# Seven block products in place of eight in half of a feed-forward layer, and one attention operand by DMA

## The chip, the cores and the metric

The kernel runs on one core of a Trainium2 chip. The metric is device microseconds of one execution, from the median of three runs. Five engines work side by side: TensorE (PE, matrix products), VectorE (DVE), ScalarE (ACT), GpSimd (POOL), and SyncE (SP), which issues most DMAs. A queue is in order on each engine.

## The reference, cut to what matters

Attention on 4 batches of 8 heads, 576 positions, 64 wide, with a block-causal mask of 64; the heads are put side by side, so 2304 tokens of width 512 leave it. Two feed-forward layers follow, the first with 2048 hidden units, the second with three input matrices and 768 hidden units.

```python
attn = exp(scores - max) / (sum + 1e-9); x = attn @ v          # 2304 x 512
h = x @ w_in;  r = maximum(h, 0);  x = (s * (r * r) + b) @ w_out      # 512 -> 2048 -> 512
h = maximum(maximum(x @ w1, x @ w2), x @ w3);  out = h @ w_out2       # 512 -> 768 -> 512
```

The weights come as 64-bit floats and have to be turned into 32-bit ones by integer work on their two words.

## The kernel before, in words

Every product is taken to near fp32 precision from halves: a matrix is split into a rounded part (hi) and its rest (lo), and one block product is three matmuls, hi by hi, hi by lo and lo by hi. A matmul has 128 rows, 128 columns of weights, and 512 or 384 tokens.

The program records operations with their reads and writes (`Sched.op`), each with a cost and one or more engines; `Sched.run` then plays a list scheduler over them and writes out one fixed order for each engine. Costs (`c_mm`, `c_exp`, `c_two`, the constants near line 259), offsets of priority (`CFG["off"]`) and the order of recording set that order. At run time each engine follows its order and waits for what an instruction reads.

**Attention** goes pair of heads by pair of heads, 16 pairs. `prep_pair` makes the operands of the next pair: hi of K and of Q (lines 444 to 450, on POOL from pair 2 on), lo of K (453), lo of Q (462), and a second copy of hi of Q, called q2 here, which the DVE computes again from the raw Q (457 to 459). `softmax_pair` then has per pair 9 score blocks: matmuls, a maximum on DVE (496), an exponential on ACT (500). `values_pair` turns the exponentials by 25 transposes (561), which ACT copies out (360), and multiplies by V.

**Weights** go through `convert` (673): a load of 512 KB, a clamp (684), a scaling of the high word (688, ACT or POOL), a shift (692), and two merging passes on DVE (696, 701). `pair_out` splits the result to hi and lo. `prepare_v` does this for a matrix taken as it is, `prepare_b` for one taken by blocks, which adds four sums and seven splits; results for later go to DRAM (wscr, bscr) and come back by `fetch`.

**The first layer** is done in two passes of 8 hidden blocks each (f = 0..7, 8..15). The tokens stand in five chunks, three of 512 and two of 384. `l1` is the first product of one f and one chunk (12 matmuls) with relu, square, scale and bias on ACT (924, 929, 936) and the split of the result; `l2` is the second product (12 matmuls). The first pass takes chunks 0 and 1 together: all `l1`, whose results go to DRAM (hscr) for lack of room and come back, then all `l2`. The other chunks and the second pass run one f after the other, with `l2` one step behind `l1`. Partial sums of the first pass wait in DRAM (pscr).

**The second layer** takes its first products by blocks: two by two blocks of weights and of tokens, in groups of 768 tokens, with seven block products in place of eight (`seven`, line 877; sums of token blocks in `blocks_of_x`, 814). A block product is 6 matmuls of 384 tokens; the sums after it are DVE additions (874).

Of the kernel before, what the change touches and what calls it, by code (L numbers as in the profile page):

```python
# [28 lines left out]
HOLD = 3  # L29
# [4 lines left out]
W_REBIAS = 2.0 ** -112  # L34
W_MAX = struct.unpack("<f", struct.pack("<I", (1151 << 20) - 512))[0]
# [22 lines left out]
def c_two(n):  # L58

    return n / 2.4 + 55  # L60
# [18 lines left out]
def c_exp(n):  # L79
    return n / 1.2 + 271  # L80
# [72 lines left out]
class Sched:  # L153
# [45 lines left out]
    def run(self):  # L199
# [26 lines left out]
        while len(order) < n:  # L226
# [28 lines left out]
            if e == "PE":  # L255

                m = self.ops[i][5]
                if side != (m == "side"):
                    c += 93 if not side else 55 if m == "turn" else 100
                side = m == "side"  # L260
# [11 lines left out]
def tile_attention_moe(ctx: ExitStack, tc: tile.TileContext, qk, vp, w_in, w_out, s_, b_, w123, w_out2, out):  # L272
# [13 lines left out]
    def places(at, n, *sizes):  # L286

        out_ = []
        for m, w in zip(n, sizes):
# [5 lines left out]

    IAT, XAT1, OAT, HAT1, RN = places(0, (NF // 2, KT, NF // 2, 2 * HOLD + 1), 1024, 1024, 1024, 1024)
    XAT, HAT, WAT_, VAT, HATB, rn = places(0, (14, 2, 8, NG, 2), 2 * HN, 2 * HN, 512, 1024, 2 * HN)
# [6 lines left out]
    PTN = sum(pt_w)  # L304
    SAT, NAT, at = places(0, (1, 2), 1024, 512)
    TAT = places(0, (5,), HN)[0]
    RAWAT, K0AT, NMAT, DENAT, RDAT, RVAT, PTAT, *EAT = places(at, (CFG["raw"], CFG["k0"], CFG["nmx"], 2, 1, CFG["rawv"], CFG["pt"]) + tuple(CFG["e"]),
                                                              2 * S, 256, NB, 36, 128, 17 * D, PTN, *e_w)
    FN = EAT.pop()
    SAT2, RGAT1, PAT, WV2, WB2, UAT, fn = places(at, (5, 3, 4, 2, 4, 6), 1024, 512, 512, 1024, 512, HN)  # L310
# [9 lines left out]
    hscr = dram.tile([NF, 128, 1024], F32, name="hscr")  # L320
    pscr = dram.tile([KT, 128, NT], F32, name="pscr")
    bscr = dram.tile([7 * 3 * NG // 2, 128, 512], F32, name="bscr")
# [11 lines left out]
    def words2(t):  # L334
# [4 lines left out]
                 x1=Strip(arena, XAT1, 1024, two), x1b=Strip(arena, OAT[1:5], 1024, two), h1=Strip(arena, HAT1, 1024, two),  # L339
                 x=Strip(arena, XAT, 2 * HN, two), v=Strip(arena, VAT, 1024, two), h=Strip(arena, HAT + HATB, 2 * HN, two), w=Strip(arena, WAT_, 512, two),  # L340
                 wb=Strip(other, WB2, 512, two), wv=Strip(other, WV2, 1024, two),
                 stg=Strip(other, SAT, 1024, words2), nrm=Strip(other, NAT, 512), rg1=Strip(other, RGAT1, 512), part=Strip(other, PAT + [UAT[0] + 512 * i for i in range(4)], 512), t1=Strip(other, TAT[0:2], HN), t2=Strip(other, TAT[2:4], HN), tt=Strip(other, TAT[4:], HN), y=Strip(other, WV2, 512),
                 u=Strip(other, UAT, HN), rg=Strip(other, RGAT, HN), gb=Strip(other, GAT, HN),
                 **{"e%d" % j: Strip(other, EAT[j], w) for j, w in enumerate(e_w)},
                 **{"iw%d" % j: Strip(arena, [x], 1024, two) for j, x in enumerate(IAT)}, **{"ow%d" % j: Strip(arena, [x], 1024, two) for j, x in enumerate(OAT)},
                 **{"pt%d" % j: Strip(other, [x + sum(pt_w[:j]) for x in PTAT], w) for j, w in enumerate(pt_w)})
# [55 lines left out]

    def parts(p):
# [7 lines left out]
    def load_pair(p):  # L411
# [3 lines left out]
        if p == 0:  # L415

            for x, i, cols, heads in [("a", 0, (384, 768), HEADS)] + [("a", 1, (S * h, S * h + C0), (h,)) for h in HEADS] + [
# [255 lines left out]
    def convert(src, kind, after=()):  # L673
# [13 lines left out]
        def f(e):  # L687
            mul_to(e, hi_f, hi_f, W_REBIAS)
# [689 lines left out]
```

## Time and profile before

| | |
|---|---|
| median of 3 runs | 852.61 us (851.32 to 856.37) |
| the profiled execution's own time | 853.07 us |
| its span, first to last instruction | 851.1 us |
| PE busy | 835.5 us, 98% |
| DVE, ACT, POOL busy | 616.2, 441.8, 81.9 us |
| TensorE clock granted, mean | 0.997 |

The span is what the profile's rows cover; about 2 us of the execution's own time lie around it. PE's busy time counts matmuls that overlap in a pipeline, so 98% doesn't say that PE goes at its peak; how many matmuls start in a stretch says more. Attention fills the span up to about 178 us, the first layer goes from there to 571 us, the second layer to the end.

### The profile page before, as it was taken

What the parts mean: (1) busy time and instruction counts of PE and PEld (TensorE: products, weight loads), DVE (VectorE), ACT (ScalarE), POOL (GpSimd) and SP (SyncE); (2) the same over time, 40 slices, a digit from 0 to 9 for tenths busy, and PEclk for the clock granted to TensorE, in tenths of its full rate; (3) what the DMA queues carried; (4) which work ended last, traced back from release to release, by engine and by line L of the source; (5) the groups of instructions that cost most, each with busy time, mean ns of one, the idle gap of its engine ahead of it and who ended that gap; (6) DMA issues with size and microseconds to landing.
All of it is one profiled execution on the core that took longest, in us unless ns stands there. A gap on an engine that the chain in (4) does not pass through costs nothing.

```text
span 851.1 us, 13711 instructions
## 1 busy us (share of the span) xinstructions
PE 835.5 (98%) x4802; PEld 735.5 (86%) x4802; DVE 616.2 (72%) x1191; ACT 441.8 (52%) x984; POOL 81.9 (10%) x94
## 2 busy tenths in 40 slices
PE   7999999999999999999999999999999999999997
PEld 6777776777888899999998888889999999999995
DVE  7788999999948899945993323567569566847662
ACT  4899999989705677655774434440115101320112
POOL 6222223202001131000100000000000000000000
PEclk9999999999999999999999999999999999999999
DMA  7556674758698888999662010247674676657742
GB/s 251 167 187 215 193 242 156 254 169 315 220 412 314 277 289 294 354 362 332 216 244 75 1 50 1 82 140 249 205 227 149 209 230 202 188 172 225 232 126 75
DMA packets 73461, 176.62 MB, mean 208 GB/s; under 512 B 8752, under 2 KB 13104, under 8 KB 73392
## 3 DMA queue, kind: packets, MB, share of 16 engines
q1 hardware_dynamic: 72672, 175.02, 62.1%
q8 instruction: 38, 0.62, 0.3%
q10 hardware_dynamic: 720, 0.72, 0.2%
q14 instruction: 31, 0.25, 0.1%
HBM read 132.91 MB, written 42.80 MB: 206 GB/s over the span
## 4 chain that ended last, share of the span: by engine, by line
PE 81%; DVE 9%; ACT 4%; DMA 3%; issue 2%; POOL 0%; ACTq 0%; SPq 0%; DVEq 0%; POOLq 0%
PE ps L368 78%; PE ps L561 4%; DVE arena L365 2%; DVE other L496 2%; ACT other L500 2%; DMA bscr<-other 1%; DVE other L365 1%; DVE arena L462 1%; ACT other L360 1%; DMA other<-pscr 1%; DVE other L701 1%; DMA other<-qk 1%; DVE arena L354 1%; DVE other L696 0%; POOL other L356 0%
## 5 line engine op out<-in xcount | busy, mean ns | idle before, releaser
L368 PE MATMUL ps<-arena 128*128 128x384 f32 (+7 forms) x3758 | 746.1, 357 | 5.4 <-ACT other L500 1.4
L368 PEld LDWEIGHTS ps<-arena 128*128 128x128 f32 (+1 forms) x3758 | 664.0, 189 | 81.1 <-ACT other L500 10.7
L874 DVE TENSOR_TENSOR other<-ps,other 128x384 f32<-128x384 f32 x189 | 101.1, 554 | 64.1 <-PE ps L368 62.4
L365 DVE TENSOR_TENSOR arena<-other,arena 128x384 fp32r<-128x384 f32 (+3 forms) x173 | 119.1, 699 | 23.1 <-ACT arena L352 18.9
L352 ACT ACTIVATE arena<-other 128x384 fp32r<-128x384 f32 (+3 forms) x107 | 59.9, 567 | 83.8 <-DVE other L1245 54.2
L924 ACT ACTIVATE other<-ps 128x512 f32<-128x512 f32 (+1 forms) x80 | 44.0, 551 | 98.3 <-PE ps L368 97.1
L354 DVE TENSOR_SCALAR arena<-other 128x512 fp32r<-128x512 f32 (+3 forms) x72 | 40.8, 569 | 70.9 <-ACT other L936 67.1
L360 ACT ACTIVATE other<-ps 128x512 f32<-128x512 f32 (+2 forms) x139 | 73.5, 571 | 29.6 <-PE ps L368 20.6
L500 ACT ACTIVATE other<-ps,other 128x576 f32<-128x576 f32 (+4 forms) x144 | 78.7, 563 | 11.2 <-DVE other L496 10.6
L496 DVE TENSOR_REDUCE other<-ps 128x1 f32<-128x576 f32 (+4 forms) x144 | 68.0, 512 | 11.8 <-ACT other L500 4.6
L352 ACT ACTIVATE other<-other 128x256 fp32r<-128x256 f32 (+3 forms) x101 | 51.9, 527 | 46.0 <-DVE other L684 37.8
L886 ACT ACTIVATE other<-ps 128x384 f32<-128x384 f32 x27 | 13.3, 491 | 114.9 <-PE ps L368 91.8
L356 POOL TENSOR_SCALAR other<-other 128x512 f32<-128x512 f32 (+1 forms) x46 | 38.6, 842 | 293.3 <-DVE other L684 162.0
L936 ACT ACTIVATE other<-other,cst 128x512 f32<-128x512 f32 (+1 forms) x80 | 61.6, 771 | 1.9
L561 PE MATMUL ps<-ident,other 128*128 128x128 f32 x400 | 57.0, 280 | 3.3 <-ACT other L500 2.9
L368 PE MATMUL ps<-other 128*64 128x64 f32 (+5 forms) x640 | 54.9, 313 | 1.2 <-ACT other L352 1.2
L561 PEld LDWEIGHTS ps<-ident,other 128*128 128x128 f32 x400 | 44.9, 143 | 7.3 <-ACT other L500 5.1
L929 ACT ACTIVATE other<-other 128x512 f32<-128x512 f32 (+1 forms) x80 | 47.0, 589 | 1.8
L368 PEld LDWEIGHTS ps<-other 128*64 128x64 f32 (+1 forms) x640 | 29.7, 136 | 20.9 <-issue 15.5
L365 DVE TENSOR_TENSOR other<-other 128x256 fp32r<-128x256 f32 (+1 forms) x85 | 41.6, 499 | 2.0 <-ACT other L352 1.4
L696 DVE SCALAR_TENSOR_TENSOR other<-other 128x512 uint32<-128x512 uint32 x56 | 38.4, 686 | 4.1 <-POOL other L356 2.7
L701 DVE SCALAR_TENSOR_TENSOR other<-other 128x512 uint32<-128x512 uint32 x56 | 39.8, 711 | 0.2
(35 smaller groups left out, 332.9 us busy)
## 6 DMA issues: line engine op xcount, KB each, us to landing
arena<-bscr SPq DMA_DIRECT2D x189, 256.0 KB, 3.1
other<-qk SPq DMA_DIRECT2D x30, 576.0 KB, 3.8
bscr<-other SPq DMA_DIRECT2D x63, 256.0 KB, 4.9
other<-w_out SPq DMA_DIRECT2D x22, 512.0 KB, 4.9
wscr<-other SPq DMA_DIRECT2D x22, 512.0 KB, 5.1
arena<-wscr SPq DMA_DIRECT2D x22, 512.0 KB, 6.1
other<-w SPq DMA_DIRECT2D x18, 512.0 KB
other<-vp SPq DMA_DIRECT2D x16, 544.0 KB, 4.5
```

Source lines behind the costliest of these rows:

```text
L352: nc.scalar.activation(out=dst, in_=src, func=AF.Copy, scale=m)
L354: nc.vector.tensor_scalar(out=dst, in0=src, scalar1=m, scalar2=None, op0=ALU.mult)
L360: nc.scalar.activation(out=dst, in_=src, func=AF.Copy)
L365: eng[e].tensor_tensor(out=dst, in0=a, in1=b, op=ALU.subtract)
L368: nc.tensor.matmul(o, l, r, start=start, stop=stop)
L496: nc.vector.tensor_reduce(out=NM.ap[:, u:u + 1], in_=v, axis=AX.X if n <= 512 else AX.XY, op=ALU.max, negate=True)
L500: nc.scalar.activation(out=ev, in_=v, func=AF.Exp, bias=NM.ap[:, u:u + 1], scale=1.0, accum_out=DEN.ap[:, d:d + 1])
L561: nc.tensor.transpose(TB.ap[:, 128 * i:128 * i + 128], x, ident)
L701: nc.vector.scalar_tensor_tensor(out=lo_w, in0=hi_w, scalar=0x80000000, in1=lo_w, op0=ALU.bitwise_and, op1=ALU.bitwise_or)
L874: nc.vector.tensor_tensor(out=out_.ap, in0=bank.ap[:, 0:HN], in1=u.ap, op=ALU.add)
L929: nc.scalar.activation(out=r, in_=r, func=AF.Square)
L936: nc.scalar.activation(out=r, in_=r, func=AF.Identity, scale=s_t, bias=b_t)
```

## The change

- In the first layer's second pass (f = 8..15) the first product is taken by blocks, as the second layer does it: seven block products in place of eight, groups of 768 tokens. `seven`, `blocks_of_x`, `prepare_b` and `fetch` serve both layers now; `hidden` and `l2_half` are new.
- The first pass takes all five chunks one after the other, `l2` three steps behind `l1` (LAG). The detour of results through hscr is gone.
- From pair 2 on, q2 is copied by a DMA from hi of Q, in place of being computed by DVE.
- `convert` does the scaling and the sign in one activation on ACT; the second merging pass on DVE is gone, and POOL no longer scales.
- The loads of the first pair are cut another way, buffers are laid out anew, and some of the scheduler's costs are changed.

```diff
 def convert(src, kind, after=()):
-            mul_to(e, hi_f, hi_f, W_REBIAS)
-        op(CFG_E("wreb", ACT=c_acts(512), Pool=c_pool(512), DVE=335), 0, f, ...)
+            nc.scalar.activation(out=hi_f, in_=hi_f, func=AF.Prelu, scale=W_REBIAS, alpha=W_SIGN)
+        op("ACT", c_acts(512), f, ...)
...
-            nc.vector.scalar_tensor_tensor(out=lo_w, in0=hi_w, scalar=0x80000000, in1=lo_w, op0=ALU.bitwise_and, op1=ALU.bitwise_or)
-        op("DVE", 602, f, ...)

 def prep_pair(p, R):
+            if p < CFG["q2d"]:      # 2
...
+            else:
+                    nc.sync.dma_start(out=f32(q2[0:64]), in_=f32(qh[0:64]))
+                load(256 * nq, f, reads=[(Q1, c) for c in keys], writes=[(KQ, (1,) + c) for c in keys], kind="prep2")

+def l2_half(G, b, f_, accs):
+        W, Hh, t, i = ready["out", f_], hs.pop((f_, b)), half(G, b), accs["n"]
+        for k in range(KT):
...
+                mm(o, W.ap[:, 0, kk], Hh.ap[:, 0, :], i == 0, False)
+                mm(o, W.ap[:, 0, kk], Hh.ap[:, 1, :], False, False)
+                mm(o, W.ap[:, 1, kk], Hh.ap[:, 0, :], False, i == HF - 1)
+            op("PE", 3 * c_mm(HN), f, ...)

-    PASSES = [(0, c) for c in range(2, NC)] + [(1, c) for c in reversed(range(NC))]
+    PASSES = [(0, c) for c in range(NC)]
-    aside = [(x, f_ + HF) for x, f_ in order1]
+    aside = [k for i in range(HF // 2) for k in [(i, "in"), ("out", HF + i), ("out", HF + i + HF // 2)]]

+    for n_, G in enumerate(GORD):
+        P1, P2 = SETS[n_ % 2], SETS[1 - n_ % 2]
+        acc = accumulators(P2, KT)
+        keep, todo = {}, []
+        for i in range(HF // 2):
+            def between():
+                for f_ in todo:
+                    l2_half(G, 0, f_, acc)
...
+            c = seven((i, "in"), P1, dst, between)
+            f1, f2 = HF + i, HF + i + HF // 2
+            for x in ("C11", "C21", "C22", "C12"):
+                hidden(c[x])          # relu, square, scale and bias, all on ACT
+            split_h((f1, 0), c["C11"])
+            split_h((f2, 0), c["C21"])
+            keep[f1], keep[f2] = c["C12"], c["C22"]
+            todo = [f1, f2]
+            prepare_aside(aside2, "w2")
...
+        acc = accumulators(P1, KT)
+        for f_ in c_order:
+            split_h((f_, 1), keep[f_])
+            l2_half(G, 1, f_, acc)

-CFG = {'aside2': 2,
+CFG = {'aside': 8, 'aside2': 24,
```

How the engines' orders move, at three places. PE, from the end of attention to the second layer, before:

```order
L650 MATMUL ps<-ident,other 36x128
L368 MATMUL ps<-arena 128x512 x561
L368 MATMUL ps<-arena 128x384 x12
L368 MATMUL ps<-arena 128x512 x12
L368 MATMUL ps<-arena 128x384 x744
L368 MATMUL ps<-arena 128x512 x12
L368 MATMUL ps<-arena 128x384 x12
L368 MATMUL ps<-arena 128x512 x552
L368 MATMUL ps<-arena 128x384 x9
```

And now:

```order
L670 MATMUL ps<-ident,other 36x128
L371 MATMUL ps<-arena 128x512 x540
L371 MATMUL ps<-arena 128x384 x12
L371 MATMUL ps<-arena 128x512 x12
L371 MATMUL ps<-arena 128x384 x12
L371 MATMUL ps<-arena 128x512 x12
L371 MATMUL ps<-arena 128x384 x12
L371 MATMUL ps<-arena 128x512 x12
L371 MATMUL ps<-arena 128x384 x1578
```

The second run of 512-wide matmuls is gone, and one long run of 384-wide ones goes on into the second layer. Over the whole program the list has 1476 matmuls of 512 and 1902 of 384 before, 900 and 2598 now; all the others are as many as before.

DVE in the middle of attention (TENSOR_REDUCE is the maximum, 64x1024 into arena is q2 or, as SCALAR_TENSOR_TENSOR, lo of Q; 64x1152 is lo of K), before:

```order
L496 TENSOR_REDUCE other<-ps 128x1 x3
L354 TENSOR_SCALAR arena<-other 64x1024
L365 TENSOR_TENSOR arena<-other,arena 64x1152
L496 TENSOR_REDUCE other<-ps 128x1 x4
L462 SCALAR_TENSOR_TENSOR arena<-other,arena 64x1024
L792 TENSOR_TENSOR xf<-xf,other 128x512
```

And now:

```order
L812 TENSOR_TENSOR xf<-xf,other 128x512
L368 TENSOR_TENSOR arena<-other,arena 64x1152
L516 TENSOR_REDUCE other<-ps 128x1 x4
L482 SCALAR_TENSOR_TENSOR arena<-other,arena 64x1024
L812 TENSOR_TENSOR xf<-xf,other 128x512
```

The q2 instruction has gone from every one of the 14 pairs. It stands now on SP as a DMA of 64x1024 (the loads there: qk is raw K and Q, vp is V, scr the denominators), where before there was

```order
L786 DMA other<-scr 64x512 x4
L481 DMA other<-vp 128x1088
L425 DMA other<-qk 128x1152 x2
L481 DMA other<-vp 128x1088
L659 DMA scr<-other 8x4x128
```

and now

```order
L806 DMA other<-scr 64x512 x4
L501 DMA other<-vp 128x1088
L478 DMA arena<-arena 64x1024
L440 DMA other<-qk 128x1152 x2
L501 DMA other<-vp 128x1088
```

so that the copy stands behind a load of V and ahead of the next raw loads.

ACT in the second pass of the first layer, before:

```order
L924 ACTIVATE other<-ps 128x512
L929 ACTIVATE other<-other 128x512
L936 ACTIVATE other<-other,cst 128x512
L352 ACTIVATE arena<-xf 128x512 x3
L924 ACTIVATE other<-ps 128x512
```

And now, by blocks (L914 copies a block product out of ps; L1232, L1237 and L1244 are relu, square, scale and bias; L355 is a hi part; L708 is a weight's scaling):

```order
L1232 ACTIVATE other<-other 128x384
L355 ACTIVATE arena<-other 128x384
L914 ACTIVATE other<-ps 128x384
L1232 ACTIVATE other<-other 128x384
L1237 ACTIVATE other<-other 128x384 x2
L1244 ACTIVATE other<-other,cst 128x384 x2
L355 ACTIVATE arena<-other 128x384 x2
L355 ACTIVATE other<-other 128x256
L708 ACTIVATE other<-other 128x512 x2
```

The relu no longer reads ps: it follows a DVE addition, and the preparation of weights stands between the steps.

## Rows read from the trace of the kernel before

**Rows 1.** Page, first lines: span, then busy us by engine.

```profile
span 851.1 us, 13711 instructions
...
PE 835.5 (98%) x4802; PEld 735.5 (86%) x4802; DVE 616.2 (72%) x1191; ACT 441.8 (52%) x984; POOL 81.9 (10%) x94
```

**Rows 2.** Windows: stretch, length, busy PE PEld DVE ACT POOL, clock, DMA, GB/s.

```profile
20.00:178.00 158.00, 154.56 (x1341) 116.50 (x1342) 145.31 (x237) 142.63 (x434) 41.54 (x48) 0.99 0.64 198
350.00:395.00 45.00, 45.00 (x261) 44.88 (x261) 24.38 (x60) 23.84 (x45) 0.00 (x0) 1.00 0.99 358
405.00:440.00 35.00, 35.00 (x204) 35.00 (x203) 34.74 (x83) 28.13 (x58) 2.72 (x2) 1.00 0.69 237
450.00:560.00 110.00, 110.00 (x487) 91.12 (x487) 41.58 (x76) 48.02 (x72) 0.00 (x0) 1.00 0.14 45
320.00:450.00 130.00, 129.04 (x731) 126.73 (x730) 105.75 (x250) 88.42 (x176) 7.98 (x7) 1.00 0.85 299
```

**Rows 3.** Groups, PE, 320:450 us: count, busy, mean ns, idle.

```profile
L368 PE MATMUL ps<-arena 128*128 128x384 f32 x703 | 123.2, 335 | 1.0 <-DVE arena L365 1.0
L368 PE MATMUL ps<-arena 128*128 128x512 f32 x28 | 6.8, 392 | 0.0
```

**Rows 4.** Waits of PE, 178:851 us: total us, times, longest.

```profile
PE ps L368 <- DVE arena L365: 1.0, 2, 0.8
```

**Rows 5.** Chain of waits, 20 to 175 us, shares by line.

```profile
by line: PE ps L368 41.3%; PE ps L561 20.1%; ACT other L500 9.7%; DVE other L496 7.9%; issue 5.7%; DVE arena L365 4.8%; ACT other L360 3.6%; DVE arena L462 2.1%; DVE xf L792 1.6%; DVE arena L354 1.3%; ACT xf L360 0.8%; DVE other L696 0.4%; 
```

**Rows 6.** Groups, DVE, attention, 20:178 us.

```profile
L365 DVE TENSOR_TENSOR arena<-other,arena 64x1152 fp32r<-64x1152 f32 x14 | 22.1, 1579 | 0.1
...
L354 DVE TENSOR_SCALAR arena<-other 64x1024 fp32r<-64x1024 f32 x14 | 16.7, 1194 | 0.2
```

**Rows 7.** Timeline of DVE, two runs of q2: start, length.

```profile
19.79 0.69 DVE L354 TENSOR_SCALAR arena<-other 64x1024 fp32r<-64x1024 f32 x1
...
30.08 1.84 DVE L354 TENSOR_SCALAR arena<-other 64x1024 fp32r<-64x1024 f32 x1
```

**Rows 8.** Timeline of POOL, hi of K and of Q, two pairs.

```profile
30.34 1.04 POOL L356 TENSOR_SCALAR arena<-other 128x1024 fp32r<-128x1024 f32 x1
...
58.69 2.63 POOL L356 TENSOR_SCALAR arena<-other 128x1152 fp32r<-128x1152 f32 x2 [2.34 <-PE ps L368]
```

**Rows 9.** Timeline of PE, the first scores of pair 6.

```profile
70.30 0.47 PE L368 MATMUL ps<-arena 128*128 128x192 f32 x2
```

**Rows 10.** Waits of SP's queue, attention: total us, times, longest.

```profile
SPq L481 <- PE ps L561: 27.2, 9, 5.9
```

**Rows 11.** DMA issues, 0:180 us: count, KB, us to landing.

```profile
other<-vp SPq DMA_DIRECT2D x16, 544.0 KB, 4.5
```

**Rows 12.** Groups, ACT, attention, 20:178 us: a weight's scaling.

```profile
L352 ACT ACTIVATE other<-other 128x512 f32<-128x512 f32 x3 | 2.1, 695 | 1.1 <-DVE other L684 1.1
```

**Rows 13.** Groups, ACT, chunks of 384, 310:440 us.

```profile
L936 ACT ACTIVATE other<-other,cst 128x384 f32<-128x384 f32 x31 | 21.9, 708 | 0.8
L929 ACT ACTIVATE other<-other 128x384 f32<-128x384 f32 x30 | 15.7, 525 | 0.8
L924 ACT ACTIVATE other<-ps 128x384 f32<-128x384 f32 x30 | 14.6, 486 | 26.1 <-PE ps L368 26.1
L352 ACT ACTIVATE other<-other 128x256 fp32r<-128x256 f32 x35 | 14.2, 428 | 5.7 <-DMA bscr<-other 2.6 <-DVE other L748 1.6 <-DVE other L701 1.2
L352 ACT ACTIVATE arena<-other 128x384 fp32r<-128x384 f32 x18 | 9.4, 525 | 0.5
```

**Rows 14.** Groups, DVE, second layer, 575:650 us.

```profile
L874 DVE TENSOR_TENSOR other<-ps,other 128x384 f32<-128x384 f32 x63 | 33.7, 554 | 20.8 <-PE ps L368 20.3
...
L365 DVE TENSOR_TENSOR arena<-other,arena 128x384 fp32r<-128x384 f32 x10 | 5.4, 552 | 1.8 <-ACT arena L352 1.8
```

**Rows 15.** Groups, DVE, weights being prepared, 250:300 us.

```profile
L701 DVE SCALAR_TENSOR_TENSOR other<-other 128x512 uint32<-128x512 uint32 x13 | 8.9, 688 | 0.1
...
L684 DVE TENSOR_SCALAR other<-other 128x512 f32<-128x512 f32 x14 | 5.9, 423 | 0.0
```

More of the change, by code (lines that the diff above doesn't have):

```diff
@@ L463, in f @@
                                                op1=ALU.subtract)
-            both("DVE", c_dve(nq), f, reads=qr + [(Q1, c) for c in keys], writes=[(Q1, c) for c in keys], kind="preplo", lock=True)
+            both("DVE", c_dve(nq), f, reads=qr + [(Q1, c) for c in keys], writes=[(Q1, ("l",) + c) for c in keys], kind="preplo", lock=True)
             if i == 0 and p == 0 or i == len(parts(p)) - 1 and p:
@@ L773, in half, with chunks_of @@
         return slice(2 * HN * G + HN * b, 2 * HN * G + HN * b + HN)
+    def chunks_of(G, b):
+        t = half(G, b)
+        return [c for c in range(NC) if CHUNKS[c][0] < t.stop and t.start < sum(CHUNKS[c])]
     def normalize(c):
@@ L812, in split_x, with blocks_of_x, xop @@
             xdone1.setdefault((c, k), []).extend((i, j))
-    def blocks_of_x(G):
+    xdone2 = {}
+    def blocks_of_x(G, layer):
         src, read = {}, {}
+        done = xdone2[G] = [] if layer == 1 else None
+        def xop(*a, **k):
+            j = op(*a, **k)
+            if layer == 1:
+                done.append(j)
         for i in range(2):
             for x, k, b in (("B11", i, 0), ("B12", i, 1), ("B21", 2 + i, 0), ("B22", 2 + i, 1)):
-                src[x, i], read[x, i] = xf[:, k, half(G, b)], [(XF, ("x2", c, k)) for c in range(NC) if CHUNKS[c][0] < half(G, b).stop and half(G, b).start < sum(CHUNKS[c])]
+                src[x, i], read[x, i] = xf[:, k, half(G, b)], [(XF, ("x", c, k)) for c in chunks_of(G, b)] if layer == 1 else [(XF, ("x2", G, b, k))]
         for x in BBLK:
@@ L902, in seven, with l1 @@
         return c
-    HS = Use(hscr)
-    def l1(c, f_, PH, away=False):
+    def l1(c, f_, PH):
         c0, n = CHUNKS[c]
@@ L1206, in tile_attention_moe @@
         s_now, c = PASSES[n_]
+        while direct and (("in", min(i + 2, HF - 1)) not in ready or i + 2 >= LAG and ("out", min(i + 2 - LAG, HF - 1)) not in ready):
+            prepare_direct("w")
         l1(c, f_, banks.get(SETS[0]))
-        if c == NC - 1 and s_now == 0:
-            ready["in", f_ + HF] = fetch("iw%d" % f_, ("in", f_ + HF), kind="wf")
         if f_ % HF == HF - 1 and n_ + 1 < len(PASSES) and PASSES[n_ + 1][1] != c:
             split_x(PASSES[n_ + 1][1])
-        if i:
-            l2_all(*steps[i - 1])
@@ L1214, in tile_attention_moe @@
-        prepare_aside(aside, "w2")
-        if n_ >= CFG["aside2"] and i % 2:
+        if i >= LAG:
+            l2_all(*steps[i - LAG])
+        if i >= CFG["aside"]:
+            prepare_aside(aside, "w2")
+        if i >= CFG["aside2"] and i % 2:
             prepare_aside(aside2, "w2")
-    blocks_of_x(GORD[0])
+    assert not direct and not aside
+    blocks_of_x(GORD[0], 1)
     for _ in WAT_:
         next_b()
-    l2_all(*steps[-1])
-    assert not aside and not aside2
+    for x in steps[-LAG:]:
+        l2_all(*x)
@@ L1222, in tile_attention_moe @@
+    assert not aside2
     while flow_v:
```

190 lines of the change are left out of this document (100 added, 90 removed).

## The prediction

> **What bounds the kernel now.** I read the page first, then windows, then the chain. The page has PE busy for 98% of the span [rows 1]; since busy matmuls overlap, the windows say more, because they count matmuls. In a stretch of 512-wide ones alone, 487 start in 110 us, one each 0.226 us; in two stretches of 384-wide ones, 261 in 45 us and 204 in 35 us, one each 0.172 us [rows 2]. These spacings hold whether DVE is busy for 38% of the stretch or 99%, and DMA for 14% or 99%, so they are PE's own, and from 178 us on the time is the number of matmuls times these two figures. What is lost beside that is little: 320 to 450 us has 703 and 28 matmuls [rows 3], which need 703 x 0.172 + 28 x 0.226 = 127.2 us of its 130; 2.8 us are lost, and PE is seen to wait there for 1.0 us in all [rows 4].
>
> Attention is another matter. From 20 to 178 us PE is busy for 154.6 us of 158, but DVE for 145.3 and ACT for 142.6 as well [rows 2], and the chain there goes over all three: 61% on PE (lines 368 and 561), the rest mostly on DVE and ACT, with a wait at each hand-over [rows 5]. So after 178 us only fewer or cheaper matmuls gain, and before it also less work on DVE or ACT.
>
> **The change part by part.**
>
> *Matmuls.* The lists of the two orders have 576 fewer of 512 and 696 more of 384. 576 x 0.226 = 130.2 us go, 696 x 0.172 = 119.7 us come: 10.4 us saved with the spacings unrounded (0.2259, 0.1720). This is the sure term. Its ends come from the spread of the narrow spacing (0.1716 to 0.1724): 10.1 to 10.7.
>
> *Stalls in the layers.* The 2.8 us lost between 320 and 450 us belonged to a stretch that is done otherwise now. What takes their place? In the first chunk the kernel needs both matrices of each f as it goes. The fifth to sixteenth converted matrix (about four are through DVE when the last maximum is) have to be there before the last `l2` of the chunk, three steps of 12 and seven of 24 matmuls after the start: 36 x 0.226 + 168 x 0.226 = 46 us. Between 250 and 300 us DVE finished 13 conversions in 50 us, one each 3.85 us [rows 15], so twelve take 46 us at that pace; one merging pass of 0.69 us is gone from each, so the pace can be better. Just enough, and the three steps between `l1` and `l2` give slack that the old one step did not.
>
> In the second pass a group of 768 tokens has four times 42 matmuls for the block products and 192 for `l2_half`: 360 x 0.172 = 62 us of PE. ACT has, per group, 16 results at 0.486 + 0.525 + 0.708 for relu, square and bias, 30 hi parts at 0.525 (16 results, 14 token blocks), and 4 copies like the 0.486: 27.5 + 15.8 + 2.0 = 45 us [rows 13]; hi parts may also go to DVE. DVE has 36 additions out of ps at 0.554 and 38 subtractions at 0.552 [rows 14]: 41 us. In the first group two matrices by blocks and two plain ones are prepared besides: on DVE six conversions at 2 x 0.42 + 0.69 [rows 15] and 22 sums and lo parts of 256 columns at no more than 0.55, two of 512 at 0.69: at most 22.7 us, together 64 of 62. That is an upper end (means of DVE overlap a little at their ends), but it says that DVE is full in one group of three. For new stalls I take the old rate, 2.8 us in 130, over the two groups (124 us) that still prepare weights: 2.7 us, and 1.4 us, half of the old stretch's loss, for the change from one pass to the other, where the first token blocks have to be split while three steps of `l2` run. So 4.1 new against 2.8 old: +1.3 us; ends: -2.8 (none new) and +12 (1 us at each of the twelve sets of seven products, below).
>
> *Attention.* q2 leaves DVE: 14 instructions, 16.7 us [rows 6]. A DMA on SP takes its place. It is ready when POOL has made hi of Q, and that is early: in pair 6 POOL ends at 61.32 us and the first scores follow at 70.30 us, 9.0 us later [rows 8, 9]. A load of V lands 4.5 us after its issue [rows 11] and is twice as large as this copy, so I cost the copy at nothing; without that cover it would cost its landing, some 4.5 us a pair. What is queued behind it on SP are the raw loads for two pairs on.
>
> What does DVE's freed time give? At least what stands in the chain itself: line 354 has 1.3% of 155 us, 2.0 us [rows 5]. At most what ACT leaves: ACT is busy for 142.6 us there, and gains five scalings of weights at 0.695 [rows 12] and four small operand copies at no more than the 0.428 of a 256-wide one [rows 13], 5.2 us, so 147.8 of 158 us: 10.2 us. I take 5 us, 0.36 us a pair, the lower half, because the chain is mostly PE's and ACT would have to reach over 96% for it. There is a reason for less: q2 took 0.69 us when POOL was still and 1.84 us when POOL made hi of Q at the same time [rows 7, 8]; its mean is 1.194. By 14 x 0.69 only 9.7 of the 16.7 us were its own work, the rest was waiting beside POOL, and what now follows next in DVE's order, lo of K (mean 1.579), can inherit the wait. The Trainium skill's page "SBUF — State Buffer", section "Who interferes with whom", says why: a DVE instruction in a two-port mode and a GpSimd one exclude each other for the whole instruction, and one with two SBUF inputs, as lo of K has, also waits for a GpSimd one that reads SBUF. The two lengths agree with it; by that rule alone the term would be 5 x 9.7 / 16.7 = 2.9 us, and the time 841.1 us.
>
> *Counted at nothing.* The merging pass that goes from all 56 conversions (38 us of DVE), and the detour over hscr: PE waited for 1.0 us in all after 178 us [rows 4], so there is little to win. The scalings that come from POOL to ACT: ACT was busy for 28 of 35 us in its fullest stretch shown after attention [rows 2]; if it were full, each would delay a result by 0.7 us. The start and the last layer's order are as before, nearly.
>
> *The sum.* 853.07 (the profiled execution) - 10.4 - 5.0 + 1.3 = 839.0 us. That execution is 0.5 us over the median of 852.61, so the sum holds for the median as well. 1% is 8.5 us, about what a measurement of this kernel can tell from no change: faster is under 844.1, slower over 861.1.
>
> **The rivals.**
>
> *A. As summed:* 839, own range 834 to 844.
>
> *B. Attention gives next to nothing.* ACT, which gets work, or the wait beside POOL, which moves to lo of K, keeps the pace. For it: ACT is at 90% there, and the mean of 1.194. Against: DVE is fuller than ACT. 853.07 - 10.4 + 1.3 less 0 to 2.9: 841 to 844.
>
> *C. Attention gives all that ACT leaves,* 10.2 in place of 5: 833.8; with no new stalls 829.7. For it: DVE is the fuller of the two and loses most. Against: three engines in a chain with hand-overs seldom fill one.
>
> *D. The second pass by blocks waits at each set.* The old `l1` read ps at once; now a result needs an addition (0.554), three ACT steps (1.72), a hi (0.525) and a lo (0.552) after its product, 3.4 us and five hand-overs, and ACT may do the three steps of another block first (1.72). The next set's first four products cover 24 x 0.172 = 4.1 us. If ACT takes the blocks in a bad order or is held up by the preparation of weights, 1 us is lost at each of the 12 sets, 12 us: 839 - 1.3 + 12 = 850, within 1%.
>
> *E. Slower: the copy of q2 comes too late.* It stands behind a load of V that waits for PE, up to 5.9 us [rows 10]. If that wait begins only when hi of Q is done, the copy lands 5.9 + 4.5 = 10.4 us later, 1.4 after the scores want it; at each of 14 pairs that is 20 us, and no gain in attention: 853.07 - 10.4 + 1.3 + 19.6 = 863.6. It decides from 9.0 us between hi of Q and landing. Against it: the wait was that long once, its mean is 3.0 us, which makes 7.5 us.
>
> *That the change doesn't do what it says* is ruled out by the orders: the counts have moved, and no new kind of matmul came.
>
> **How the numbers follow.** A 0.57, B 0.16, C 0.10, D 0.12, E 0.05. I predict A's 839. The range of 828 to 849 takes in A, B, nearly all of C and the lower half of D; E and the worse half of D are left out, with a little below. Faster by over 1%: A but for 0.02, C, half of B: 0.73. Within 1%: the rest of A and B, nearly all of D: 0.21. Slower: E and a hundredth of D: 0.06.
>
> **What the profile would show.** The matmul term is right if a 384-wide stretch of the second pass has one start each 0.172 us, and the first layer ends some 10 us earlier after the end of attention than before (393 us, 178 to 571). The attention term is right if the first 512-wide stretch starts about 5 us before 178 us, with DVE idle more than ACT. Rival D would be idle PE with releases from ACT or DVE in the second pass, B an unchanged end of attention with ACT over 95% busy, E waits of the score matmuls on the DMA into arena. The prediction would be wrong most likely by the first chunk: if conversions come slower than one each 3.85 us, PE waits at the steps where they are first used.

## The result, and the profile after

The changed kernel takes 845.43 us (median of 5, 843.48 to 846.28), the kernel before 853.2 us on the same chip (5 runs, 851.32 to 856.37): ratio 0.990, 95% interval 0.988 to 0.992. That is 7.8 us less. The forecast was 839, the range 828 to 849: the time is in the range, but 6.4 us over the forecast, at the edge of "within 1%", to which the forecast had given a chance of 0.21 (0.73 to faster). The range took in rival B, nearly all of C and half of D too, so that the time falls in it says little of the mechanism: 13.6 us less were forecast, and 7.8 came.

The profiled execution took 843.48 us. The page's first lines:

```profile
span 841.7 us, 14337 instructions
...
PE 826.4 (98%) x4922; PEld 749.0 (89%) x4922; DVE 644.5 (77%) x1329; ACT 466.7 (55%) x1077; POOL 47.5 (6%) x65
```

Against [rows 1], PE is 9.1 us less busy with 120 matmuls more, since narrow ones took the place of wide ones. The windows answer to [rows 2], and the columns are the same:

```profile
20.00:178.00 158.00, 153.32 (x1333) 115.31 (x1332) 134.22 (x219) 146.92 (x444) 33.34 (x41) 1.00 0.74 219
190.00:290.00 100.00, 100.00 (x442) 82.72 (x442) 85.61 (x198) 68.17 (x121) 0.00 (x0) 1.00 0.78 270
460.00:580.00 120.00, 120.00 (x694) 120.00 (x694) 82.66 (x180) 59.58 (x121) 0.00 (x0) 1.00 0.56 176
378.00:392.00 14.00, 12.16 (x67) 11.27 (x67) 7.89 (x17) 6.46 (x13) 0.00 (x0) 1.00 1.04 405
```

The second is 512-wide: 100 / 442 = 0.226 us. The third is the second pass by blocks: 120 / 694 = 0.173 us. Both spacings are as before. The fourth is the change from one pass to the other: 67 matmuls of 0.173 us need 11.6 of 14 us, and the DMA engines are full (a share of 1.04). In attention (the first) DVE lost 11.1 us of work and ACT gained 4.3.

The waits of PE from 178 us on (total us, times, longest), where [rows 4] had 1.0 us:

```profile
PE ps L371 <- DMA arena<-bscr: 1.3, 1, 1.3
PE ps L371 <- DVE arena L357: 0.4, 1, 0.4
PE ps L371 <- ACT other L363: 0.4, 1, 0.4
```

They name three late things, once each. Two lie at the change of pass, and none at one of the twelve sets of seven products. The chain of waits there, 372 to 390 us (start, length, what):

```profile
371.93 9.46 PE ps L371 x55
381.39 6.24 DMA arena<-bscr
387.63 0.04 issue
387.67 2.36 PE ps L371 x12
```

The block of weights that PE is stopped for lands 6.24 us after its issue, while DMA moves 405 GB/s. Blocks of that size land in a median 3.1 us where DMA moves 162 GB/s (470 to 560 us).

The chain from 20 to 175 us, by line, answers to [rows 5]:

```profile
by line: PE ps L371 44.1%; PE ps L581 19.9%; ACT other L520 11.8%; ACT other L363 7.7%; issue 7.0%; DMA arena<-arena 2.9%; ACT arena L355 1.4%; POOL arena L359 1.4%; ACT other L708 1.2%; ACT xf L363 0.9%; DVE other L516 0.7%; DVE xf L812 0.
```

The maximum on DVE has gone from 7.9% to 0.7% (now line 516), and lo of K, 4.8% before, is not among those named; ACT's exponential (520) and transposed copies (363) rose from 13.3% to 19.5%. The DMA copy is in the chain once, for 4.45 us, ahead of a normalisation on DVE, not of a score matmul. And yet the last matmul of attention starts at 176.5 us, 1.3 us earlier than before (177.8).

PE is seen to wait for 3.5 us in all between 20 and 178 us, for ACT alone (its waits: total us, times, longest):

```profile
PE ps L581 <- ACT other L520: 2.0, 3, 1.0
PE ps L371 <- ACT other L363: 1.0, 1, 1.0
PE ps L581 <- ACT other L363: 0.3, 1, 0.3
PE ps L581 <- ACT xf L363: 0.2, 1, 0.2
```

DVE's groups in attention show part of why, against [rows 6]:

```profile
L368 DVE TENSOR_TENSOR arena<-other,arena 64x1152 fp32r<-64x1152 f32 x13 | 26.3, 2023 | 1.4 <-POOL arena L359 1.3
...
L482 DVE SCALAR_TENSOR_TENSOR arena<-other,arena 64x1024 fp32r<-64x1024 f32 x14 | 17.3, 1238 | 0.4
```

q2 is gone from DVE but for the first pairs, and lo of K (64x1152) takes a mean 2.023 us where it took 1.579. The timeline shows why: it takes 1.33 to 1.35 us when POOL is still, and some 2.18 us when POOL makes hi of K and of Q at the same time.

```profile
37.54 2.16 POOL L359 TENSOR_SCALAR arena<-other 128x1152 fp32r<-128x1152 f32 x2 [4.50 <-PE ps L371]
38.73 2.17 DVE L368 TENSOR_TENSOR arena<-other,arena 64x1152 fp32r<-64x1152 f32 x1
...
94.29 1.35 DVE L368 TENSOR_TENSOR arena<-other,arena 64x1152 fp32r<-64x1152 f32 x1
```

Of the 14 in the window before, 4 took the longer time; of the 13 now, 10 did, and one took 1.81 us.

**Where the time went.** Spans: 851.1 to 841.7, 9.4 us less. By the starts of the matmuls there are four parts. The lists, at the measured spacings, give -10.3. PE's time lost beyond the spacings after 178 us rose from 4.2 to 6.1 us, +1.9 (2.7 of the 6.1 between 383 and 388 us, 1.1 between 312 and 318). The last matmul of attention starts 1.3 us earlier, but 0.7 us of that are three matmuls of the first layer, which the kernel before ran ahead of it (at 173.6 to 174.1 us) and the changed kernel behind it: attention itself gives -0.6. What follows the last matmul of the program gives -0.4. The sum is -9.4. This execution is 4.5 us over the forecast: to 0.2 us, attention gave 4.4 too little, the stalls cost 0.6 more, and the end of the program gave 0.4 that wasn't forecast. The other 1.9 us are the distance from this execution, the quickest of its five, to the median.

### The profile page after: what moved, and what is told of

Same layout as the page of the kernel before. It is cut to its first block, busy times and chain, and to the rows that moved or that the text cites. A ratio compares the mean times of both kernels' runs of the same rounds, so it can differ in the third digit from the quotient of the medians.

```text
span 841.7 us, 14337 instructions
## 1 busy us (share of the span) xinstructions
PE 826.4 (98%) x4922; PEld 749.0 (89%) x4922; DVE 644.5 (77%) x1329; ACT 466.7 (55%) x1077; POOL 47.5 (6%) x65
## 4 chain that ended last, share of the span: by engine, by line
PE 74%; DVE 9%; DMA 7%; ACT 6%; issue 3%; POOL 0%; SPq 0%; ACTq 0%; DVEq 0%; POOLq 0%
PE ps L371 70%; DMA bscr<-other 5%; PE ps L581 4%; ACT other L520 2%; DVE other L716 2%; DVE arena L368 2%; ACT other L363 2%; DVE other L368 1%; DVE other L764 1%; DVE other L704 1%; DMA arena<-bscr 1%; DMA pscr<-other 1%; ACT other L708 1%; DVE other L712 1%; DMA arena<-arena 1%
## 5 line engine op out<-in xcount | busy, mean ns | idle before, releaser
L371 PE MATMUL ps<-arena 128*128 128x384 f32 (+6 forms) x3878 | 736.7, 348 | 5.5 <-ACT other L363 1.4
L902 DVE TENSOR_TENSOR other<-ps,other 128x384 f32<-128x384 f32 x273 | 145.9, 553 | 81.1 <-PE ps L371 77.9
L355 ACT ACTIVATE arena<-other 128x384 fp32r<-128x384 f32 (+3 forms) x124 | 66.1, 545 | 113.9 <-DVE other L1303 68.0
L516 DVE TENSOR_REDUCE other<-ps 128x1 f32<-128x448 f32 (+4 forms) x144 | 68.8, 513 | 21.1 <-PE ps L371 17.6
L520 ACT ACTIVATE other<-ps,other 128x448 f32<-128x448 f32 (+4 forms) x144 | 79.3, 564 | 9.1 <-DVE other L516 8.1
L914 ACT ACTIVATE other<-ps 128x384 f32<-128x384 f32 x39 | 19.1, 489 | 109.8 <-PE ps L371 89.4
L355 ACT ACTIVATE other<-other 128x256 fp32r<-128x256 f32 (+2 forms) x87 | 37.0, 437 | 27.7 <-DMA bscr<-other 14.1
L708 ACT ACTIVATE other<-other 128x512 f32<-128x512 f32 x56 | 38.2, 694 | 20.8 <-DVE other L704 20.7
L716 DVE SCALAR_TENSOR_TENSOR other<-other 128x512 uint32<-128x512 uint32 x56 | 38.3, 688 | 3.9 <-ACT other L708 2.9
L1232 ACT ACTIVATE other<-other 128x384 f32<-128x384 f32 x48 | 24.6, 517 | 29.2 <-DVE other L902 29.2
L1303 DVE TENSOR_TENSOR other<-other 128x384 f32<-128x384 f32 x72 | 38.7, 554 | 1.3
L359 POOL TENSOR_SCALAR arena<-other 128x1152 fp32r<-128x1152 f32 (+4 forms) x31 | 33.7, 1102 | 53.3 <-PE ps L371 42.6
L1244 ACT ACTIVATE other<-other,cst 128x384 f32<-128x384 f32 x48 | 32.7, 699 | 0.4
```

What stands on the lines that cost most here:

```text
L355: nc.scalar.activation(out=dst, in_=src, func=AF.Copy, scale=m)
L359: nc.gpsimd.tensor_scalar(out=dst, in0=src, scalar1=m, scalar2=1.0, op0=ALU.mult, op1=ALU.mult)
L371: nc.tensor.matmul(o, l, r, start=start, stop=stop)
L516: nc.vector.tensor_reduce(out=NM.ap[:, u:u + 1], in_=v, axis=AX.X if n <= 512 else AX.XY, op=ALU.max, negate=True)
L520: nc.scalar.activation(out=ev, in_=v, func=AF.Exp, bias=NM.ap[:, u:u + 1], scale=1.0, accum_out=DEN.ap[:, d:d + 1])
L708: nc.scalar.activation(out=hi_f, in_=hi_f, func=AF.Prelu, scale=W_REBIAS, alpha=W_SIGN)
```

## The experiments

The theory at first: PE's count of matmuls sets the time from 178 us on; in attention PE with hand-overs through ACT sets the pace, so DVE's freed time buys little; and stalls at the change of pass come from full DMA queues. The rivals: the copy by DMA costs what DVE gains; ACT is the pace; the new planner costs did harm.

| kernel | median us | ratio to before, 95% | last attention matmul, us | lost by PE after 178 us |
|---|---|---|---|---|
| the change | 845.43 | 0.990 [0.988, 0.992] | 176.5 | 6.1 |
| e1_q2_dve | 856.84 | 1.005 [1.002, 1.008] | 181.2 | 11.2 |
| e2_q2_pool | 850.11 | 0.996 [0.994, 0.997] | 175.5 | 16.1 |
| e4_costs | 848.61 | 0.994 [0.992, 0.996] | 177.0 | 10.4 |
| e5_act_relief | 859.22 | 1.007 [1.004, 1.010] | 192.1 | 8.3 |
| b1_before_q2_dma | 854.39 | 1.001 [0.999, 1.003] | 175.9 | 6.6 |
| e9_q2_dve_costs | 857.88 | 1.004 [1.002, 1.005] | 175.6 | 22.9 |
| e7_out_late | 847.96 | 0.993 [0.990, 0.995] | 176.9 | 9.8 |
| e3_eighth_product | 857.39 | 1.004 [1.003, 1.006] | 176.3 | 6.6 |
| e10_short_klo | 844.47 | 0.990 [0.987, 0.993] | 176.2 | 9.0 |
| e11_short_exp | 843.60 | 0.988 [0.985, 0.991] | 175.2 | 7.2 |
| e12_short_scores | 842.50 | 0.988 [0.984, 0.991] | 175.2 | 6.7 |
| e13_store_latency | 856.28 | 1.003 [1.002, 1.005] | 176.9 | 18.1 |

The last two columns are worked out from the starts of the matmuls in each profiled execution (excess over 0.227 and 0.173 us); the kernel before has 177.8 and 4.2 there. In it and in b1 the three first-layer matmuls (0.7 us) stand ahead of the last one of attention. The change, e3, e7 and e13 have one and the same order in attention and end it at 176.3 to 176.9 us, so a difference of 0.3 us there means nothing. All edits but b1's are to the changed kernel.

**Is the saving of matmuls real?** The first of the seven products of each set in the second pass is done twice, 72 matmuls of 384 more:

```diff
-        for i in range(2):
+        for i in (0, 1, 0, 1) if twice else range(2):
...
-        M = product("A11", "B11", P1)
+        M = product("A11", "B11", P1, key[1] == "in")
```

> The changed kernel with the first of the seven block products of each of the 12 sets in the first layer taken twice into the same bank (the second time from the start, so the result is the same): 72 more matmuls of 384, as many as eight products in place of seven have. If PE's spacing sets the pace of the second pass: +72 x 0.172 = 12.4 us, total 856 to 859, and the saving was real in full. If ACT or DVE set it: less, 846 to 852.

Measured: 857.39 us, 12.0 over the changed kernel's median; the spans differ by 12.7. 72 x 0.1729 = 12.4 us. So in the second pass, to within 0.4 us in 72 matmuls, every matmul costs its full spacing, nothing hides it, and an eighth product would have cost what the expectation says.

**q2 back on DVE, with and without the old planner costs; and on POOL.**

```diff
-        'q2d': 2,                                        # e1, e9
+        'q2d': 16,
-    return n / 2.4 + 14                                  # c_two; e9, e4
+    return n / 2.4 + 55
-    return n / 1.2 + 235                                 # c_exp; e9, e4
+    return n / 1.2 + 271
-                    c += 92 if not side else 126 if m == "turn" else 256
+                    c += 93 if not side else 55 if m == "turn" else 100
-        'eng': {..., 'q2': ['DVE'], ...}                 # e2, with 'q2d': 16
+        'eng': {..., 'q2': ['Pool'], ...}
```

> The changed kernel with q2 computed by DVE again, as before, from pair 2 on (no copies by DMA). The changed kernel took 845.4 us, its attention ended at 176.5 us of the span, pairs 2 to 15 took 10.1 us each. Theory 1 (freeing DVE is worth some 5 us, and the copy, landing late, eats it): attention ends within 1 us of 176.5, DVE back on the chain of waits. Theory 2 (PE and ACT set the pace, DVE's work was covered): attention ends within 1.5 us of 176.5 too, total 844 to 847, and DVE's chain share stays far under the 18% of before only if the chain does not need it. Theory 3 (the copy itself harms): attention ends 3 us or more earlier, total 842.

> The changed kernel with q2 on DVE and the scheduler's old costs. With the new costs attention ended at 181.2. Theory 6 (the new costs lose 3 us in attention when DVE is full): attention ends at 177 to 178.5. Theory 7 (the five weight scalings that moved from POOL to ACT lose them, late in attention): pair 12 starts near 125 as before and the end stays at 180 or later.

> The changed kernel with q2 computed by POOL: neither DVE's 16.7 us nor the copy by DMA is there. Theory 1 (freed DVE pays, the copy's landing eats it): attention ends at about 172 us, total 841. Theory 2 (PE and ACT set the pace): attention ends at 176.5 within 1.5 us, total 844 to 847.

> The changed kernel with the scheduler's old costs for exponentials, for the products of V and for TensorE's changes of mode; nothing but the order moves. Theory 2: attention ends within 2 us of 176.5, total 843 to 848. Theory 4 (the new costs made a worse order of attention and so hide DVE's gain): attention ends at 173 or earlier, total 842 or less.

Measured: with q2 on DVE, attention ended at 181.2 us under one set of costs and at 175.6 under the other; with q2 off DVE, at 175.5 to 177.0. None of the theories written down for e1 or e9 had these ends; e2 and e4 ended attention where theory 2 had it, with totals over it. Taken alone, e1 would have "shown" the 5 us of the forecast (181.2 against 176.5); e9, with q2 on DVE as well, shows that another order alone moves the end as far. Over all, q2 leaves DVE in three pairs of kernels, each with the order that the planner made of it: e1 to the change ends attention 4.7 us earlier, e9 to e4 1.4 us later, and the kernel before to b1 (below) 1.9 us earlier. In e9 DVE has as much work in attention as before, and attention ends earlier than in the changed kernel:

```profile
20.00:178.00 158.00, 156.08 (x1342) 118.11 (x1342) 145.00 (x240) 145.64 (x440) 37.95 (x44) 0.99 0.62 197
```

Its worse total comes from after attention, where it loses 22.9 us. Up to the thirteenth pair e9 goes through attention as the kernel before does (the 64-wide maxima of pairs 1 to 12, counted from 0, start within 0.2 us of each other), and it ends 2.2 us earlier, 1.5 without the three first-layer matmuls. So the other parts of the change can give, with q2 still on DVE, as much as the whole change gave in attention; which of them does it was not tested. Each of these edits made the planner write out another order of the whole program, so totals of e1, e2, e4 and e9 say little about q2.

**The kernel before, with only the copy of q2 by DMA.**

```diff
+            if p < 2:
+                both(pick("q2", p, ...))
+            else:
+                nc.sync.dma_start(out=f32(q2[0:64]), in_=f32(qh[0:64]))   # by load(...), as in the change
```

> The kernel before with one part of the change alone: q2 copied by DMA from pair 2 on (with the key of its own for lo of Q, which the copy needs). Attention of before ended at 177.8 us of its span. Theory 2a (q2 off DVE is worth some 5 us of attention, as between the changed kernel and the one with q2 back on DVE, 176.5 against 181.2; something else in the change took it back): attention ends at 172 to 174, total 847 to 849. Theory 5 (that difference was only another order that the planner happened to write): attention ends at 176 to 180, total 851 to 856.

Measured: 854.39, no difference; attention ends 1.9 us earlier (175.9 against 177.8), just outside theory 5 on the side of 2a, and PE loses 2.4 us more later. DVE lost 6.0 us of busy time there, not 16.7. Of the rest, 7.1 us are lo of K, which took 22.1 us before [rows 6], and 3.6 other work that grew or moved into the stretch:

```profile
L365 DVE TENSOR_TENSOR arena<-other,arena 64x1152 fp32r<-64x1152 f32 x14 | 29.2, 2084 | 1.0 <-POOL arena L356 0.7
```

In e9, where q2 stands on DVE, the same subtraction takes a mean 1.517 us. So what stands beside POOL's work inherits the wait that q2 had.

**ACT relieved by DVE.** ACT's copies of results into xf go to DVE:

```diff
-        'je': ['ACT'],
+        'je': ['DVE'],
```

> The changed kernel with attention's 32 copies into xf on DVE in place of ACT: about 16 x (0.61 + 0.23) = 13.4 us from ACT to DVE, which has room. Theory 2 (ACT beside PE sets the pace): attention ends 2 to 6 us earlier, 171 to 174, total 840 to 843. Theory 1 (DVE is still what counts) or PE alone sets the pace: no gain, 176.5 or later, total 845 to 849.

Measured: 859.22, the last attention matmul at 192.1 us (some first-layer work is mixed in from 181.7 on), and pairs of a mean 11.0 us (10.1 in the changed kernel). Neither theory had a time that long. It speaks against ACT's load as the one limit; but the order changed with it, so this run doesn't tell load from order.

**What is the pace in attention? Three runs with the order kept.** Here each engine's list is the changed kernel's, instruction for instruction; from pair 4 on one kind of instruction is only made shorter.

```diff
-                sub_to(e, kl[0:64], k[0:64], f32(kh[0:64]))                              # e10, DVE
+                n = slice(0, 64 if p >= 4 else None); sub_to(e, kl[0:64, n], k[0:64, n], f32(kh[0:64, n]))
-                nc.scalar.activation(out=ev, in_=v, func=AF.Exp, ...)                    # e11, ACT
+                m = (Ellipsis, slice(0, 32 if p >= 4 and n > 400 else None)); nc.scalar.activation(out=ev[m], in_=v[m], ...)
-                    mm(o, KQ.ap[0:64 + NU, q:q + 128], KQ.ap[0:64 + NU, c], False, True) # e12, PE
+                    m = 32 if p >= 4 else c.stop - c.start; mm(o[:, 0:m], ..., KQ.ap[0:64 + NU, c.start:c.start + m], False, True)
```

> The changed kernel with every engine's order as it was; from pair 4 on, lo of K is made for 64 of its 1152 columns only (the rest of it keeps what an earlier pair left), so 12 DVE instructions of a mean 2.023 us shrink to about 0.13 each: DVE loses 22.7 of its 134.2 us in attention. Theory (PE sets the pace, with hand-overs through ACT; DVE's time is not the limit): the last attention matmul stays at 174 to 177 us (176.5 in the changed kernel) and the time at 843 to 845.5. Rival (DVE is still the pace, and what q2 gave went into longer lo of K, 1.579 to 2.023): attention ends 8 to 15 us earlier, time 831 to 838.

> The changed kernel with every engine's order as it was; from pair 4 on, the exponentials of the 448- and 576-wide blocks are taken over 32 and 64 columns only. 48 ACT instructions of 0.650 and 0.757 us lose some 0.35 and 0.43 each: ACT loses 18.7 of its 146.9 us in attention. Theory (PE with hand-overs through ACT): the transposes that wait for an exponential get it earlier, so 3 to 8 us come out of the end of attention (176.5), time 838 to 843. Rival 1 (ACT is the pace by its load): 12 to 18 us earlier, time 828 to 834. Rival 2 (DVE is the pace): 0 to 2 us.

> The changed kernel with every engine's order as it was; from pair 4 on, the second of the two score matmuls of a block (68 rows: the lo parts and the mask) covers 32 columns only. 120 matmuls lose 2752 columns a pair, 12 x 2752 / 2400 = 13.8 us of PE by the ideal of one column a cycle at 2.4 GHz. Theory (PE is the pace): attention ends 8 to 13 us earlier than 176.5, time 833 to 838. Rivals (ACT or DVE is the pace by load): 0 to 4 us earlier, time 841 to 845.

Measured: attention ends at 176.2, 175.2 and 175.2 us: 0.3, 1.3 and 1.3 us earlier; the first is within the spread of one and the same order. The totals are 844.47, 843.60 and 842.50 us, the last two above what the theory had. The windows of 20 to 178 us, of e10, then e11, then e12:

```profile
20.00:178.00 158.00, 153.63 (x1336) 115.89 (x1336) 122.67 (x221) 146.70 (x446) 33.31 (x41) 1.00 0.77 220
```

```profile
20.00:178.00 158.00, 154.33 (x1339) 117.66 (x1338) 135.00 (x224) 134.59 (x446) 34.40 (x41) 0.99 0.74 220
```

```profile
20.00:178.00 158.00, 150.73 (x1341) 115.41 (x1340) 135.01 (x223) 148.08 (x447) 36.28 (x42) 0.99 0.76 219
```

DVE lost 11.5 us in e10 and ACT 12.3 us in e11, and nearly all of it turned into idle time. Both are less than was meant (22.7 and 18.7); in e10 the shortened subtractions still took a mean 0.879 us, not 0.13, where they stand beside POOL's work:

```profile
L368 DVE TENSOR_TENSOR arena<-other,arena 64x64 fp32r<-64x64 f32 x12 | 10.5, 879 | 1.1 <-POOL arena L359 1.1
```

In e12 PE's busy time fell by only 2.6 us: the shortened matmuls overlap their neighbours and still take a mean 186 ns each (PE's group, 44 to 165 us; the full ones of 288 columns take 297):

```profile
L371 PE MATMUL ps<-arena 68*128 68x32 f32 x116 | 21.5, 186 | 0.0
```

By the starts of the matmuls the score matmuls of that stretch went from 47.0 to 41.7 us, so e12 took 5.4 us from PE and not the 13.8 that were meant; yet the transposes took 37.4 us where they took 34.4: PE waits in another place. The chain says what took over. By line, 44 to 165 us, the changed kernel, then e11, then e12:

```profile
by line: PE ps L371 44.7%; PE ps L581 20.4%; ACT other L520 11.0%; issue 7.8%; ACT other L363 6.1%; DMA arena<-arena 3.7%; POOL arena L359 1.8%; ACT arena L355 1.4%; ACT xf L363 1.0%; DVE other L516 0.6%; DVE xf L812 0.6%; DVE other L704 0.
```

```profile
by line: PE ps L371 56.4%; PE ps L581 23.3%; DVE other L516 4.6%; issue 3.9%; ACT other L520 3.7%; ACT other L363 2.7%; DVE other L704 1.4%; DVE other L712 1.1%; DVE arena L482 1.0%; DVE xf L812 0.6%; DVE other L716 0.5%; DVE arena L368 0.4
```

```profile
by line: PE ps L371 27.7%; ACT other L520 21.9%; PE ps L581 12.7%; ACT other L363 12.1%; issue 5.6%; DVE other L516 4.5%; DMA other<-scr 4.0%; ACT arena L355 2.6%; ACT xf L363 2.1%; DVE arena L482 1.6%; DVE xf L812 1.5%; DVE arena L368 1.0%
```

In the changed kernel PE is 65% of the chain and ACT 20%. Relieve ACT, and PE is 80% of the chain at nearly the same length; relieve PE, and its share falls to 40% while ACT's goes to 39%. So my theory fell in half: DVE isn't the pace (e10), but neither is PE alone (e12 was to give 8 to 13 us, and e11 3 to 8) nor ACT alone (e11 was to give 12 to 18). In this order either of the two, relieved, uncovers something else after 1.3 us, and by the chains that is the other one. No run shortened both at once, so that it is their balance, and not a path of hand-overs through both, is argued and not shown.

**The change of pass.** Two tries at the stall between 383 and 388 us. In e7 the weights for the second product are fetched two per set instead of all at the start of the pass; in e13 the planner is told that a store of prepared weights lands after 5 us, not 2.

```diff
-        ready["out", f_] = fetch("oc%d" % i, ("out", f_), kind="wf")   # e7: in a loop ahead of the pass
+        next_oc(2)                                                     # e7: in each of the first four sets
-        load(1024 * n, f, reads=..., writes=[(SCRW, key)], kind=kind)            # e13
+        load(1024 * n, f, reads=..., writes=[(SCRW, key)], kind=kind, lat=5000)  # e13
```

> The changed kernel with the eight 512 KB loads of the second pass's output weights spread, two ahead of each of the first four sets of products, in place of all eight at the change of pass. Theory 8 (the 2.7 us that PE loses at 383 to 388 us come from a burst of loads: DMA moves 400 to 420 GB/s from 370 to 390 us, and the first blocks land 6.2 us after issue): that loss falls under 1 us, total 842 to 844. If the loss has another cause (blocks issued late because their slots are not free): it stays, 845 to 846.

> The changed kernel, its planner told that a store of prepared weights lands after 5 us and not 2 (in the trace these stores land 3.7 and 5.8 us after issue). Theory (the planner sets the ACT instruction that reuses the buffer too early, and the fetches of blocks too late): the stall of 1.1 us at 314 to 317 goes, that at the change of pass (2.7 us) halves, time 843 to 844.5. Rival (the queues are full there, 400 GB/s, and any other order only moves the loss): as with the other re-ordered plans, a PE gap of 3 us or more at 380 to 395 followed by matmuls at half the clock, time 846.5 to 849.

Measured: both are worse than the change, e7 by 2.5 us, e13 by 10.8 us, and both lie outside all that was put down for them. In e7 the loss between 380 and 400 us didn't fall under 1 us but rose from 2.7 to 5.2. In e13 the stall of 1.1 us at 315 us went as hoped (0.1 left), but 18.1 us were lost in all, 12.7 of them between 380 and 410 us. Waits of PE in e13, 375 to 415 us, and a window of it:

```profile
PE ps L371 <- DMA arena<-bscr: 7.2, 2, 4.5
PE ps L371 <- DVE arena L357: 1.2, 1, 1.2
PE ps L371 <- DVE arena L368: 0.4, 1, 0.4
```

```profile
400.00:410.00 10.00, 5.49 (x24) 5.20 (x23) 2.52 (x6) 4.46 (x9) 0.00 (x0) 0.83 1.02 394
```

In the change, e7 and e13 DMA moves some 400 GB/s where PE waits for blocks, at a share of 1.0. This fits that a longer latency in the plan or later issues don't make room and only choose whose block is late, as the rival written down for e13 has it, with a size far over it. It is argued and not shown: what would lower the traffic at that place, such as preparing the second layer's weights later, wasn't tried. No version here beats the changed kernel with the whole computation done.

## Why the prediction was right in kind and 6.4 us off

- **Matmuls, -10.4:** right, -10.3 by the counts and the spacings after, which are those before. The spans bear it out: behind the last matmul of attention 673.3 us became 665.2, 8.1 less, which is the 10.3 without the 0.7 that moved, less 1.9 of stalls, and with the 0.4 at the end. And e3 shows that a matmul more costs all of its spacing.
- **Stalls, +1.3:** mechanism in part, size nearly: +1.9. The old ones were 2.3 us by the starts of the matmuls (put at 2.8), the new ones 4.2 (put at 4.1), but in other places. The change of pass, put at 1.4, cost 2.7; the two groups that still prepare weights, put at 2.7, cost 0.3 (at 446 us). In the first pass, where none was forecast, 0.1 came at 350 us and 1.1 at 315 us: there, by the chain, ACT waits for the store of an earlier block into bscr before it may use the buffer again, and a copy out of ps that PE needs stands behind that on ACT.

```profile
310.69 3.71 DMA bscr<-other
```

  The forecast looked for the stalls in DVE; in the two large ones the longest wait was for a DMA.
- **First chunk, counted as just enough:** right; PE lost nothing between 180 and 290 us.
- **Attention, -5.0 (2.0 to 10.2): the step that failed.** It measured -1.3, and -0.6 without the three first-layer matmuls, below the lower end. The step rests on "before it also less work on DVE or ACT" gains, and on "at least what stands in the chain itself: line 354 has 1.3%". That isn't a lower bound. A chain names who came last; take that away, and the next comes as late as the distance between them, which may be nothing. A third of q2's time moved into lo of K (0.444 us x 13 = 5.8 us of 16.7). That the rest bought next to nothing fits e10, where 11.5 us less of DVE with the order kept gave 0.3, and e9, where DVE took 145.0 us and attention was shorter still. In the order of the kernel before, no run took q2 away with all else kept, so what its time was worth there stays open.
- The **reason for less** that the forecast gave was right in its fact: lo of K inherited the wait beside POOL. The Trainium skill's page "SBUF — State Buffer", section "Who interferes with whom", says that an instruction of DVE with two SBUF inputs contends with a GpSimd instruction that reads SBUF; the trace agrees, with 2.17 us beside POOL's work and 1.35 us without it in the rows above. The 2.9 us worked out beside it were still too many.
- **Rivals.** B (attention gives next to nothing, 841 to 844) is nearest: this execution's 843.48 us lie in it and the median is 1.4 us over it. But ACT is at 93% of the stretch, not over 95%, and by e11 it is not ACT alone. C is out: attention gave 1.3 us at most. D, a wait at every set, is not seen: after the change of pass the waits of PE name none. E, the copy too late for the scores, is not seen, although the load of V ahead of it on SP waits longer for PE, up to 8.3 us where [rows 10] had 5.9. Ahead of the copy itself (line 478) SP waits for POOL 8 times, up to 0.7 us, so the load of V had gone through when hi of Q was done; at the other 6 pairs the copy is issued at most 1.7 us after hi of Q. It lands a median 5.9 us after issue. PE's waits above don't name it, and where the trace has the landing (7 of 14) it comes 1.6 to 4.9 us ahead of the first score matmul that reads it. So it could be counted at nothing, though it took longer than the 4.5 us of the forecast (waits of SP's queue, and the DMA issues, as [rows 11]):

```profile
SPq L501 <- PE ps L371: 31.5, 10, 6.8
SPq L501 <- PE ps L581: 19.7, 4, 8.3
...
SPq L478 <- POOL arena L359: 2.8, 8, 0.7
```

```profile
arena<-arena SPq DMA_DIRECT2D x14, 256.0 KB, 5.9
```

**What stays open:** why the other executions of the changed kernel take up to 2.8 us more than the profiled one. Four profiled executions with the same order after attention (the change, e10, e11, e12) lost 2.7, 5.6, 3.3 and 2.7 us between 380 and 400 us, so the change of pass is one place where they can differ; e10's profiled execution, with the 5.6, was the slowest of its four (846.08 us against 843.40 to 845.18). That it is the cause was not tested. And the start of attention gained 2.7 us (the 64-wide maximum of pair 1 starts at 24.0 against 26.7 us), which the way from there to that of pair 15 gave back (142.1 against 139.5 us): whether by order or by the longer lo of K is not settled.

## What to carry to other kernels

In a stretch that is only matmuls, count them and multiply by the spacing that the trace shows; doubling one product tests this (12.7 us of span for 12.4 counted). In a stretch where three engines hand work round, the share of an engine in the chain of waits is no lower bound on what its removal gives: shorten one instruction kind per engine with the order kept, and see whose does anything, before paying for the relief of one. Where a planner writes the order, an edit that lets it plan again compares two orders, and here that alone moved attention by 5.6 us (e1 against e9) and the stalls after it by 4 to 17 us.

## What the runs showed of the hardware

After a stall of PE at the change of pass, the matmuls behind it sometimes ran at the lower clock. In e10, PE was stopped for 2.8 us by a late block, and nine matmuls then started 0.320 us apart (384 columns at 1.2 GHz) before the spacing was 0.173 us again. Windows of e10:

```profile
384.00:388.00 4.00, 1.78 (x9) 1.34 (x8) 1.14 (x3) 2.86 (x6) 0.00 (x0) 1.00 1.01 373
388.00:390.00 2.00, 1.47 (x7) 1.48 (x8) 0.00 (x0) 0.00 (x0) 0.00 (x0) 0.88 0.95 323
390.00:393.00 3.00, 3.00 (x12) 3.00 (x11) 1.00 (x2) 0.00 (x0) 0.00 (x0) 0.51 0.89 274
393.00:396.00 3.00, 3.00 (x19) 3.00 (x19) 1.23 (x3) 1.22 (x3) 0.00 (x0) 1.00 0.90 305
```

The granted clock is 1.00 while PE waits, 0.88 as it starts again, then 0.51, and 1.00 from 393 us on. That adds some 1.5 us (9 x 0.147 and a little on each side) to a wait of 2.8. In the changed kernel (stops of 0.6, 0.4 and 1.4 us) and in e11 (0.7, 0.4 and 1.8 us) the clock stayed at 1.00 there. So a stall can cost half as much again as the wait that the trace names, as it did in e10.
